# Loading the rests of strided tensors in pairs instead of one by one, in an attention and spectral mix kernel

## The chip, the core and the metric

The kernel runs on one core of a Trainium2 chip. A core has a matrix engine (TensorE, "PE" in the profile, its weight loads "PEld"), three engines for element-wise work (VectorE "DVE", ScalarE "ACT", GpSimd "POOL"), a queue engine (SyncE "SP") and 16 DMA engines that move data between the device memory and the on-chip memory. The metric is the device time of one execution in microseconds (us). Less is better.

## The reference

Three inputs q, k and v of 8 batches x 8 heads x 576 positions x 64 go through sparse attention. Heads 0 to 3 see a local window of 32 positions, heads 4 to 7 the earlier positions with the same remainder by 32 ("strided"):

```python
rel = pos[:, None] - pos[None, :]
mask_local = (rel >= 0) & (rel < stride)
mask_strided = (rel >= 0) & (pos[None, :] % stride == pos[:, None] % stride)
...
attn_out = softmax(masked scores) @ v
```

The result, taken as x of 8 x 576 x 512, is mixed along the positions in the frequency domain, with a complex 512 x 512 matrix for each of 64 modes, and then goes through a channel mix:

```python
X = np.fft.rfft(x, axis=1)
Yr = Xr @ w_r - Xi @ w_i      # for each of 64 modes
Yi = Xr @ w_i + Xi @ w_r
y = np.fft.irfft(Y, n=S, axis=1)
u = x + y
return u + np.maximum(u @ w_ch, 0.0)
```

The weights w_r and w_i are 2 x 64 x 512 x 512 numbers of four bytes, 134 MB; they are most of what is read.

## The kernel before

All loads of q, k, v and of the weights are issued from POOL's queue, in one order that the program writes out by hand; they turn four-byte numbers into two-byte ones on the way. The small constants come in over the queues of ACT and SP, and the output leaves over SP's, its last two pieces over ACT's.

The work has these stages:

1. Strided attention, batches 0 to 7 (loop at L751). Before batch b's scores, POOL issues some later loads: strided tensors with `load_str` (L219), local tensors with `load_loc` (L239), weights with `w_fetch` (L174). While a batch's scores and values run, `str_front` turns the next batch's q, k and v (L275, L291).
2. Local attention, batches 0 to 7 (loop at L780). Between its pieces stand the first 64 passes of the spectral mix, `mode(0, m)` (L542), which use one half of the channels.
3. The second half of the spectral mix, `mode(1, m)` for m from 0 to 57 (loop at L848), with pieces of the channel mix between the modes: `turn` (L588), `premix` (L637) and, by the sixteens, `spec` (L837).
4. The last six modes (loop at L959), then the tail: the rows of the output by `v_rows` and `u_rows`, summed on DVE and POOL and stored.

A strided tensor of one batch is 72 rows of 2048 numbers: 18 blocks for each of four heads, with the heads outermost. It lies in the on-chip buffer `ring`, in one of 12 slots: three tensors (v, q, k) for each of four batches. `load_str` loads them in pieces. The first 64 rows go in one transfer, for one batch (L229) or for two batches at once (L227). The remaining 8 rows, the "rest", are loaded for two batches when the even one is loaded. That makes twelve pairs of rests: v, q and k of batches 0 and 1, of 2 and 3, of 4 and 5, of 6 and 7. The condition at L233 counts them: the first five (v, q, k of batches 0 and 1, v and q of 2 and 3) are loaded as one transfer of 8 x 2 rows (L234), the other seven as two transfers of 8 rows (L237).

The weights of two modes come in two transfers, one for w_r and one for w_i, 128 rows of 2048 numbers each (L196); the last four modes come one by one (L199), as does one half of w_i for mode 0. There are five buffers for them in turn, and three more in places that other tensors take over. A pass of `mode` (L553) waits for its weights, and its fetch of later weights waits for a buffer. A transfer on POOL's queue is also issued only when the one eight places before it has landed.

Of the kernel before, what the change touches and what calls it, by code (L numbers as in the profile page):

```python
# [79 lines left out]
def kernel(  # L80
# [10 lines left out]
    nc = tc.nc  # L91
# [118 lines left out]
    SLOT = {2: 0, 0: 1, 1: 2}  # L210
# [8 lines left out]
    def load_str(b, nb):  # L219
        for vi in (2, 0, 1):  # L220
            n = 3 * (b % 4) + SLOT[vi]
            two = ring[:, n : n + 4 : 3, :]
            src = SRC[vi][b - b % 2 : b - b % 2 + 2, 4:8].rearrange(
                "b h (c r) d -> (h c) b (r d)", r=32
            )
            if nb == 2:
                nc.gpsimd.dma_start(two[0:64], src[0:64])  # L227
            else:
                nc.gpsimd.dma_start(ring[0:64, n, :], src[0:64, b % 2])  # L229

            if b % 2 == 0 and 3 * (b // 2) + SLOT[vi] < 5:  # L233
                nc.gpsimd.dma_start(two[64:72], src[64:72])  # L234
            elif b % 2 == 0:
                for j in range(2):
                    nc.gpsimd.dma_start(two[64:72, j], src[64:72, j])  # L237

    def load_loc(*bs):  # L239
        for b in bs:  # L240
# [461 lines left out]

    psum_pools(tp=3, sc=3, av=2)
    load_str(0, 1)
    const_load(nc.scalar, "cI", "cM6", "cM5", "cFs")
    load_str(1, 1)
    const_load(nc.sync, "cMl", "cFl", "cA")
    load_str(2, 2)
    w_fetch()

# [260 lines left out]
    for i in range(len(units)):  # L971
        v_rows(i)
        b, t = units[i]
# [42 lines left out]
```

## Time and profile before

| what | value |
| --- | --- |
| three runs, us | 439.85, 440.37, 439.7 (median 439.85) |
| the profiled execution, us | 439.85 |
| its span, first to last instruction, us | 438.1 |
| mean granted TensorE clock | 0.831 |
| busy: PE, DVE, ACT, POOL | 76%, 49%, 43%, 30% |
| moved by the DMA engines | 92.16 MB, 29107 packets |
| read from device memory | 163.22 MB |
| rests alone (L237) | 14 transfers of 32 KB, 6.5 to 15.0 us to landing, 11.2 in the median |
| rests in pairs (L234) | 5 transfers of 64 KB, 5.8 to 9.6 us to landing, 7.4 in the median |
| weights (L196) | 122 transfers of 512 KB, about 19 us to landing |

The profile cuts the span into 40 equal slices of 10.95 us. "GB/s" counts bytes as they are written, so half of what is read for the converted tensors. The line of DMA gives the mean busy share of the 16 engines in tenths. A landing is when all sixteen engines have reported that their part of a transfer is done; the trace keeps the time of each report, without the number of its engine. A line in the chain of waits names what was going on in the step that ended last: `DMA wt<-in_moe_w_i_dram` is a transfer of weights on its way, `PE y L553 x16` sixteen matmuls of a mode.

### The profile page before, as it was taken

How to read it: one execution, taken by the hardware profiler on the slowest of the kernel's cores; microseconds unless marked ns; L12 is line 12 of the kernel's file. 1: busy time of each engine (PE TensorE's matmuls, PEld its weight loads, DVE VectorE, ACT ScalarE, POOL GpSimd, SP SyncE). 2: the span in 40 equal slices, each digit the busy share in tenths (PEclk: the TensorE clock that was granted, in tenths of full speed). 3: DMA queues.
4: the chain of work that ended last, by engine and by line, in shares of the span. 5: the costliest groups of instructions: out<-in, count | busy, mean ns of one | idle time of the engine just before them, and what ended most of it. 6: DMA issues, size and time to landing. Idle time of an engine off the chain costs nothing.

```text
span 438.1 us, 12090 instructions
## 1 busy us (share of the span) xinstructions
PE 335.0 (76%) x5298; PEld 241.3 (55%) x5298; DVE 215.3 (49%) x466; ACT 188.1 (43%) x353; POOL 132.5 (30%) x215
## 2 busy tenths in 40 slices
PE   1986978779885878788874648577676859999994
PEld 1865766667664666666653335355444546655441
DVE  2788778844423243433511034335534535753895
ACT  1686678635442344345441302023322402442883
POOL 6433343323322222222222222222222222210893
PEclk9999899869786588788875558698978868989999
DMA  8999999999999999999999999999999999991687
GB/s 175 207 211 213 211 198 197 197 190 211 209 212 203 214 213 215 213 214 213 214 211 210 214 214 214 214 214 213 213 214 213 214 213 214 214 196 29 264 314 285
DMA packets 29107, 92.16 MB, mean 210 GB/s; under 512 B 4160, under 2 KB 5184, under 8 KB 29056
## 3 DMA queue, kind: packets, MB, share of 16 engines
q0 software_dynamic: 24816, 81.28, 95.0%
q1 hardware_dynamic: 3440, 9.46, 5.8%
q10 hardware_dynamic: 800, 0.67, 0.6%
q8 instruction: 41, 0.67, 0.6%
q14 instruction: 10, 0.08, 0.1%
HBM read 163.22 MB, written 9.44 MB: 394 GB/s over the span
## 4 chain that ended last, share of the span: by engine, by line
DMA 69%; PE 19%; DVE 5%; ACT 2%; issue 2%; POOL 1%; DVEq 0%; POOLq 0%
DMA wt<-in_moe_w_i_dram 49%; DMA wt<-in_moe_w_r_dram 10%; DMA ring<-in_k_dram 4%; DMA ring<-in_v_dram 3%; PE sc L651 3%; DMA ring<-in_q_dram 3%; PE y L553 3%; PE u L694 2%; PE v L694 2%; PE v L897 2%; DVE xb L256 1%; DVE kz L298 1%; PE tp L401 1%; PE tp L659 1%; ACT X L266 1%
## 5 line engine op out<-in xcount | busy, mean ns | idle before, releaser
L553 PE MATMUL y<-X,wt 128*128 128x16 f16 (+1 forms) x2048 | 82.3, 192 | 66.4 <-DMA wt<-in_moe_w_i_dram 65.2
L553 PEld LDWEIGHTS <-wt 128*128 128x128 f16 (+1 forms) x2048 | 72.4, 103 | 78.8 <-issue 56.2
L196 POOL DMA_DIRECT2D wt<-in_moe_w_r_dram x62 | 36.5, 588 | 131.1 <-PE y L553 51.0
L196 POOL DMA_DIRECT2D wt<-in_moe_w_i_dram x60 | 35.3, 588 | 75.4 <-DMA wt<-in_moe_w_i_dram 54.8
L660 ACT ACTIVATE v<-sc 128x512 f16<-128x512 f32 x32 | 19.1, 597 | 81.8 <-PE sc L651 81.7
L651 PE MATMUL sc<-w_cp,xT 128*128 128x512 f16 (+1 forms) x160 | 51.2, 445 | 1.8 <-DVE xT L623 1.8
L477 ACT ACTIVATE PL<-sc 128x480 f16<-128x480 f32 (+1 forms) x48 | 27.5, 579 | 50.7 <-PE sc L463 50.4
L255 DVE RECIPROCAL rec<-av 90x4 f32<-90x4 f32 (+2 forms) x80 | 14.6, 183 | 47.0 <-PE av L492 35.6
L256 DVE TENSOR_TENSOR xb<-av,rec 90x256 f16<-90x256 f32 (+2 forms) x80 | 36.0, 450 | 2.8
L661 DVE COPY xo<-tp 128x512 f16<-128x512 f16 x32 | 22.1, 692 | 29.9 <-PE tp L659 29.9
L408 DVE COPY qT<-tp 128x576 f16<-128x576 f16 x16 | 12.0, 757 | 41.4 <-PE tp L401 38.5
L401 PE MATMUL tp<-cI_s,ring 64*64 64x64 f16 x864 | 27.1, 213 | 2.5 <-issue 1.9
L266 ACT ACTIVATE v<-tp 128x640 f16<-128x640 f16 (+1 forms) x24 | 19.4, 807 | 21.8 <-PE tp L435 18.6
L366 ACT ACTIVATE PL<-sc 90x360 f16<-90x360 f32 (+1 forms) x48 | 22.8, 490 | 7.0 <-PE sc L359 6.1
L401 PEld LDWEIGHTS <-ring 64*64 64x64 f16 x864 | 21.3, 126 | 7.6 <-issue 4.8
L929 DVE TENSOR_TENSOR osb<-u,rl 128x512 f32<-128x512 f32 x36 | 23.6, 688 | 2.6 <-PE u L694 1.3
L603 DVE COPY xT<-tp 128x512 f16<-128x512 f16 x16 | 11.0, 689 | 28.1 <-PE tp L597 15.0
L266 ACT ACTIVATE kz<-tp 64x360 f16<-64x360 f16 (+1 forms) x32 | 19.0, 593 | 11.5 <-PE tp L401 10.1
L912 POOL TENSOR_TENSOR rl<-rl,xo 128x512 f32<-128x512 f32 x16 | 18.3, 1159 | 18.2 <-ACT rl L910 17.9
L447 PE MATMUL sc<-cMl_s,cI_s 128*128 128x480 f16 (+1 forms) x48 | 22.5, 469 | 1.6 <-ACT X L266 1.6
L651 PEld LDWEIGHTS <-xT 128*128 128x128 f16 (+1 forms) x160 | 14.5, 108 | 16.2 <-issue 4.6
L463 PE MATMUL sc<-qT,kz 128*128 128x160 f16 (+1 forms) x160 | 22.4, 267 | 0.3 <-issue 0.3
(106 smaller groups left out, 655.7 us busy)
## 6 DMA issues: line engine op xcount, KB each, us to landing
wt<-in_moe_w_r_dram POOLq DMA_DIRECT2D x62, 512.0 KB, 18.9
wt<-in_moe_w_i_dram POOLq DMA_DIRECT2D x60, 512.0 KB, 19.4
out_dram<-osb SPq DMA_DIRECT2D x14, 512.0 KB, 2.7
ring<-in_v_dram POOLq DMA_DIRECT2D x8, 288.0 KB, 13.9
ring<-in_q_dram POOLq DMA_DIRECT2D x8, 288.0 KB, 13.8
ring<-in_k_dram POOLq DMA_DIRECT2D x8, 288.0 KB, 13.4
ring<-in_v_dram POOLq DMA_DIRECT2D x3, 512.0 KB, 14.6
ring<-in_q_dram POOLq DMA_DIRECT2D x3, 512.0 KB, 14.6
```

The source lines that it names most:

```text
L196: nc.gpsimd.dma_start(dst, rows)
L256: nc.vector.tensor_tensor(out=dst, in0=val.rearrange("p h (q c) -> p h c q", c=4), in1=rec[0:n, 0:pieces] .to_broadcast((n, pieces, 64)) . ...
L266: nc.scalar.activation(out=out, in_=in_, func=ACTF.Copy)
L366: nc.scalar.activation(out=PS[0:n, ds(POFF[t], 4 * n)], in_=scp[0:n, 0 : 4 * n], func=ACTF.Exp, scale=SCALE,)
L401: nc.tensor.transpose(tp[ds(64 * hp, 64), ds(64 * i, 64)], qn[ds(64 * hp, 64), ds(64 * (9 * g + i), 64)], idn[ds(64 * hp, 64), ds(64 * hp, ...
L447: nc.tensor.matmul(scp[:, 0 : n * times].rearrange("p (h x) -> p h x", h=times), idn, mask_rows("cMl", n, times), start=True, stop=False,)
L463: nc.tensor.matmul(scp[:, ds(col, n)], kzs[par][:, hp, ds(s0, 128)], qTs[par][:, ds(s0, n)], start=False, stop=(i == len(todo) - 1),)
L477: nc.scalar.activation(out=dst, in_=src, func=ACTF.Exp, scale=SCALE)
L553: nc.tensor.matmul(yv[:, mi, e, :], wt[pr, XC[c], ds(128 * e, 128)], Xh[half][pr, c, :, :, m], start=(c == 0), stop=(c == 3),)
L651: nc.tensor.matmul(vp[pr, :], xT[:, ch, cols], w_chs["cp"][:, ch, :], start=(ch == 0), stop=(ch == 3),)
L661: nc.vector.tensor_copy(out=xo[pr].rearrange("p (h q c) -> p h q c", h=2, c=4), in_=tp[pr, 0:512].rearrange("p (h c q) -> p h q c", h=2, c=4),
L929: nc.vector.tensor_tensor(out=osb[:, t % 2, :], in0=up, in1=rls[b, t][:, t % 2, :], op=AluOp.add)
```

## The change

`load_str` no longer loads any rests one by one: each of the twelve pairs is one transfer of 8 x 2 rows. For the first five nothing changes. For the other seven (k of batches 2 and 3, and v, q and k of 4 and 5 and of 6 and 7) one instruction on POOL's queue stands where two stood. The rows and their places in `ring` are the same, and so is the order of all other instructions on every engine.

```diff
@@ -227,14 +227,8 @@
                 nc.gpsimd.dma_start(two[0:64], src[0:64])
             else:
                 nc.gpsimd.dma_start(ring[0:64, n, :], src[0:64, b % 2])
-            if b % 2 == 0 and 3 * (b // 2) + SLOT[vi] < 5:
+            if b % 2 == 0:
                 nc.gpsimd.dma_start(two[64:72], src[64:72])
-            elif b % 2 == 0:
-                for j in range(2):
-                    nc.gpsimd.dma_start(two[64:72, j], src[64:72, j])
```

## The prediction

> **What bounds the kernel now.** I read the page from the top, then the chain of waits in order of time, then the moved bytes around the changed transfers. The page:
>
> ```profile
> PEclk9999899869786588788875558698978868989999
> DMA  8999999999999999999999999999999999991687
> GB/s 175 207 211 213 211 198 197 197 190 211 209 212 203 214 213 215 213 214 213 214 211 210 214 214 214 214 214 213 213 214 213 214 213 214 214 196 29 264 314 285
> q0 software_dynamic: 24816, 81.28, 95.0%
> q8 instruction: 41, 0.67, 0.6%
> DMA 69%; PE 19%; DVE 5%; ACT 2%; issue 2%; POOL 1%; DVEq 0%; POOLq 0%
> ```
>
> POOL's queue q0 keeps the 16 DMA engines at 9 tenths or more until slice 35, at a flat 214 GB/s: the stream of weights paces the kernel. The chain says until when (start, length, what):
>
> ```profile
> 319.70 19.38 DMA wt<-in_moe_w_i_dram
> 339.36 20.34 DMA wt<-in_moe_w_i_dram
> 359.83 0.64 PE y L553 x16
> ...
> 376.04 0.86 PE sc L651 x4
> ...
> 387.12 1.71 PE sc L651 x4
> ```
>
> Before 359.83 each step is a landing; after it TensorE hardly waits. Its waits from 360 on hold one for a weight, and that one ends at 359.83:
>
> ```profile
> PE y L553 <- DMA wt<-in_moe_w_i_dram: 2.9, 1, 2.9
> ```
>
> So the time is when the weights issued at 339.36 have landed, plus 78 us of TensorE, VectorE and ScalarE work. Anything that brings that landing forward shortens the kernel, as long as the last weights also come earlier.
>
> **Who lands last.** A transfer has landed when all its engines are done, and the trace holds sixteen stamps for each, one per DMA engine. I sorted those of the strided loads of batches 6 and 7 into the earlier and the later eight (us):
>
> ```
>                       issued   first eight      last eight
> v, 64 rows a batch     44.67   55.84 - 57.05    58.05 - 59.26
> v, rest, batch 6       46.66   56.02 - 57.22    58.35 - 59.55
> v, rest, batch 7       47.18   56.19 - 57.38    58.67 - 59.85
> q, 64 rows a batch     47.70   58.38 - 59.59    61.16 - 62.31
> k, rest, batch 7       59.55   61.26 - 62.35    64.88 - 66.09
> weights                60.05   65.12 - 65.60    67.39 - 68.52
> ```
>
> From one 64-row transfer to the next the last eight take 3.11 us (58.05 to 61.16), the first eight 2.54. The packet records show why: of a rest loaded alone (8 rows) eight engines carry one 4 KB packet each, the other eight only the 4-byte stamp, and it is the same eight (call them A, the others B) for both rests of a pair and for v, q and k. Back to back, a row costs its engine 0.305 us and a stamp behind a row 0.022. Six pairs of rests (twelve rows) put A behind B by 12 x (0.327 - 0.01) = 3.8 us; the means of the two eights at the last rest's stamps differ by 3.74, so the halves were level at 23 us.
>
> For a pair loaded as one (L234), the packets of the second and third pair (q and k, batches 0 and 1) show eight engines with two rows each, and for the third pair the other eight: they alternate. Level at 23 us is what this gives if A is the half of pairs 2 and 4: 4 rows, plus 2 for the first rests alone, against 6.
>
> Two more things decide the end. First, B has run dry once, since POOL could not issue: each issue waits until the transfer eight places earlier has landed, which A delays.
>
> ```profile
> 54.70 0.61 POOL L227 DMA_DIRECT2D ring<-in_k_dram  x1 [2.25 <-DMA wt<-in_moe_w_r_dram]
> 56.86 0.52 POOL L237 DMA_DIRECT2D ring<-in_k_dram  x1 [1.56 <-DMA wt<-in_moe_w_i_dram]
> 59.55 0.51 POOL L237 DMA_DIRECT2D ring<-in_k_dram  x1 [2.17 <-DMA ring<-in_v_dram]
> 60.05 0.61 POOL L196 DMA_DIRECT2D wt<-in_moe_w_r_dram  x1
> ```
>
> The moved bytes from 56 to 70 us, in 0.35 us steps, sag at 60.5 to 63.5:
>
> ```profile
> GB/s 211 258 211 211 199 199 199 199 211 234 222 222 187 141 129 187 141 152 199 152 187 199 211 187 187 258 234 211 199 246 187 176 208 214 221 206 222 204 190 223
> ```
>
> The gap of the means falls from 3.74 to 2.70 by the weights' stamps: B lost 1.04 us there. Second, each of the 41 instruction fetches on q8 (16 KB) sets one engine back by about 1.35 us, in a round of eight engines. Followed from stamp to stamp, two of them are in A and six in B. Relative to the quickest engine, the transfer that ends the wait at 359.83 has A's two at 7.82 and 6.43 us and the latest of B at 5.47; in the last transfer of the stream (393.00 to 399.10) A's two stand at 6.10 and 5.70, the latest of B at 4.90. One engine of A sets the end.
>
> **The change, part by part.** In seven pairs (k of batches 2 and 3, all of 4 to 7) two POOL transfers of 8 rows become one of 2 x 8 rows. Bytes, rows, the order of all other instructions and the queues of SP and ACT stay. Removed: seven issues on POOL's queue.
>
> - POOL's time: 7 x about 0.52 us (rows of L237), against 7 x about 0.08 more for the wider issue (0.60, row of L234). POOL is 30% busy and waits for landings around these lines (rows above), so this is worth nothing by itself.
> - A: 14 x 0.327 = 4.58 us go; with alternation going on, pairs 6, 8, 10 and 12 fall to A, 4 x 0.61 + 7 x 0.022 = 2.59 come. Net -1.98. If the seven began on B, A would get three: -2.6.
> - B: 3 x 0.61 + 0.15 - 0.14 = +1.84; with four pairs +2.45. The dry spell goes if it comes from A's lag and the places the rests take: -1.04; at the other end it stays: 0. I take -1.04, since the issues just before it wait for landings 2.2 us each, and two transfers in place of three then stand in the same eight places. So +0.80, bounds +0.80 and +2.45.
> - A pair lands when two rows of one engine are in, not one: 0.305 us later on its eight. The first compute that such a load holds up is L275 on q of batch 6, released at 62.64 by A's last stamp. By alternation that pair falls to B, which by then has carried three pairs: 59.94 + 6 x 0.305 = 61.8. So it comes earlier, not later, and the lag on A covers the wider pair.
>
> Sum at 359.83: A 7.82 - 1.98 = 5.84, B 5.47 + 0.80 = 6.27: the latest engine moves from 7.82 to 6.27, so 1.55 earlier, and B is now last. At the stream's end: A 4.12, B 5.70 against 6.10, 0.40 earlier; TensorE starts the last mode at 400.14, 1.04 after its weights landed, so it can start up to 1.44 earlier. The smaller counts: -1.45. The profiled execution took 439.85 us (span 438.1, 1.75 around it), which is also the median of the three runs: 438.4.
>
> [...]
>
> **The rivals.**
>
> *The gain stays in B.* B takes four pairs, or its dry spell stays. Then B at 359.83 is 5.47 + 1.41 = 6.88 (four pairs) or 7.31 (three, dry): 0.94 or 0.51 earlier; at the end 0.83 or 0.40 after the slack of 1.04: 439.0 or 439.45. Both together: 7.92 and 7.35, so 0.1 to 0.2 late: 440.05. For it: B has six of the engines that fetches delay. Against: the gap fell just where the bytes sag.
>
> *Slower: the granted clock in the last 78 us.* TensorE is busy 39.9 of the 42 us from 360 to 402, at a mean clock of 0.90 there (0.75 from 106 to 360). The chain shows the price: four L651 passes take 1.71 us at half clock (387.12) and 0.86 at full. A half-clock stretch of the clock record, 3.4 us, costs 1.7 us. From two such stretches more the change loses: +3.4 - 1.45 = +1.95, 441.8; one more gives 440.1. For it: the clock drops in short stretches all along, and moved work meets them elsewhere. Against: the work itself is the same, and three runs agree within 0.7 us.
>
> *A's lag alone counted.* If B's fetches fall elsewhere or B gains more, the full 1.98 arrives: 437.9.
>
> *The rests are not what they seem*, that is, a pair is again carried as single rows on A: no row changes its engine, only seven stamps go: 439.7. The second and third pair speak against it.
>
> **How the numbers follow.** Forecast, 437.7 to 439.2 around 438.4: 0.43. Gain kept by B or the pair carried as before, 438.9 to 440.2: 0.30. Full gain: 0.07. Slower by the clock, from 440.8: 0.20. The three runs span 0.15%, so I call 0.2% (0.88 us) the least that can be told from no change: faster is below 438.97, slower above 440.73. Faster: 0.40 of the forecast, 0.07, 0.02 of B's case: 0.49. Slower 0.21, the rest 0.30. The range, 437.0 to 441.0, takes in every case but the two-stretch clock and stray gains there.
>
> **What would show it.** Right: the later eight no longer fall behind through the strided loads (the two halves within 1 us at 61 us instead of 3.74); no sag below 190 GB/s at 60 to 63; the wait at L553 that ended at 359.83 ends near 358.3; the last weights land near 398.7. Wrong in its first step if the halves still part by 3 us; in its second if the sag stays; in its third if the landing comes earlier and TensorE's work after it takes longer than 78 us, with more half-clock stretches. A landing later than 359.7 would break the whole argument.

## The result, and the profile after

| | before | after |
| --- | --- | --- |
| median, us (runs) | 439.79 (439.7 to 440.37, 4) | 434.65 (433.94 to 435.15, 4) |
| ratio after to before, 95% interval | | 0.9879 (0.9861 to 0.9897) |
| profiled execution, us; its span | 439.85; 438.1 | 434.99; 433.2 |
| TensorE's wait for the weights of a mode ends, us | 359.83 | 355.07 |
| from there to the end of the span, us | 78.3 | 78.1 |
| last weights landed, us | 399.10 | 394.32 |

The change saves 5.3 us (4.5 to 6.1 by the interval), over three times the forecast 1.45. The direction was right, the size far off: 434.65 lies under the range.

The page of the changed kernel, the lines that answer to the first ones of the prediction:

```profile
PEclk9999799958997565985965559597969688989999
GB/s 174 203 210 214 213 213 211 212 210 212 214 213 213 213 213 214 213 214 214 214 212 213 213 214 213 214 214 213 214 213 214 213 214 213 213 193 37 267 318 288
q0 software_dynamic: 24704, 81.28, 94.7%
DMA 59%; PE 26%; DVE 7%; issue 3%; ACT 3%; POOL 0%; DVEq 0%; POOLq 0%
```

As many bytes, 112 packets fewer (seven stamps on sixteen engines). The row to read is GB/s: slices 6 to 9 (55 to 99 us) now stand at 213 211 212 210, where they were 198 197 197 190. From slice 14 on the two rows nearly agree. The chain of waits around the landing that sets the end (start, length, what):

```profile
315.79 19.48 DMA wt<-in_moe_w_i_dram
335.27 0.28 issue
335.55 19.38 DMA wt<-in_moe_w_i_dram
354.93 0.14 issue
355.07 0.64 PE y L547 x16
```

It has the same shape as before, 4.76 us earlier. TensorE's one wait for a weight from 355 to 402 us is as long as it was (L547 is the L553 of before):

```profile
PE y L547 <- DMA wt<-in_moe_w_i_dram: 3.1, 1, 3.1
```

And the moved bytes from 56 to 70 us have lost their sag:

```profile
GB/s 211 211 211 199 211 234 246 199 211 211 176 199 222 246 211 211 211 199 199 199 234 234 222 187 211 211 187 246 234 222 187 206 195 238 207 203 187 208 211 211
```

Where the time came from is read off a table by stages: a stretch, its length, the busy times of PE, PEld, DVE, ACT and POOL with the instructions they began, then PE's granted clock, the DMA engines' busy share and GB/s. The kernel before, then the changed one:

```profile
60.00:62.70 2.70, 1.13 (x23) 0.79 (x20) 2.38 (x7) 1.62 (x4) 1.25 (x3) 1.00 0.98 168
62.70:106.00 43.30, 36.44 (x741) 30.30 (x742) 28.81 (x70) 26.39 (x54) 15.01 (x27) 0.88 1.12 198
106.00:140.00 34.00, 24.75 (x537) 19.91 (x534) 11.43 (x22) 12.95 (x26) 9.79 (x17) 0.80 1.09 208
140.00:355.00 215.00, 157.14 (x2654) 113.23 (x2653) 78.52 (x160) 71.25 (x127) 50.58 (x86) 0.75 1.07 213
```

```profile
60.00:62.70 2.70, 2.38 (x45) 1.73 (x42) 2.56 (x7) 2.44 (x6) 1.05 (x3) 1.00 1.05 209
62.70:106.00 43.30, 35.84 (x718) 29.36 (x718) 29.60 (x74) 26.09 (x55) 13.46 (x25) 0.84 1.09 211
106.00:140.00 34.00, 26.19 (x620) 21.11 (x618) 13.40 (x26) 16.00 (x30) 10.70 (x19) 0.92 1.07 213
140.00:355.00 215.00, 160.29 (x2628) 114.71 (x2626) 78.64 (x161) 68.99 (x123) 50.70 (x86) 0.72 1.06 213
```

By rates: 2.7 x (1 - 168/209) = 0.5 us in the dry spell, 43.3 x (1 - 198/211) = 2.7 us in the stage in which local tensors (L244, in the changed kernel L238) and weights are loaded in turn, 34 x (1 - 208/213) = 0.8 us behind it: 4.0 of the 4.76 us by 140 us, nothing afterwards. The rest is where the last engine stands beside the mean: at the landing that ends the wait, the last of the sixteen stamps is 4.0 us behind their mean before and 3.4 after. So most of the gain lies in a stage that the change doesn't touch at all: the last transfer that it edits is issued at 59.55 us before and at 51.56 after.

The busy share of the DMA engines is the clue: before, they were busier in that stage (1.12 against 1.09) and moved less. A packet itself took longer. The records of single packets show it. An undisturbed 4 KB packet (a row of weights or of a strided tensor) takes 324 ns, a packet of 2304 bytes (a local tensor's) 192 ns. From 65 to 140 us, counted as slow above 400 and 250 ns:

```
                 4096 bytes       2304 bytes       excess over 324 / 192 ns
before           240 of 1933      278 of 3072      5.05 us an engine
after              9 of 2107       17 of 3072      0.20 us an engine
```

All 3072 packets of 2304 bytes fall into this window in both kernels. Of the 4 KB packets 174 fewer got through before: 0.71 MB, or 3.3 us of the stream at 213 GB/s. (Both traces hold all 17984 of them, so none is missing.) The slow packets come in bouts of one to 2.5 us in which nearly all engines are slow at once, at 70, 73 to 75.5, 79 to 81, 88 to 90 and 93 to 95.5 us. Between 74 and 75 us the median is 522 ns for 4 KB and 335 ns for 2304 bytes, and all engines together move 146 GB/s. All bouts fall into stretches where one half of the engines, two to four microseconds ahead, is already on the next kind of row. But not all of such a stretch is slow: from 67 to 69, 71 to 73 and 77 to 79 us packets of both kinds also run side by side, and 7 of 418 are slow. What had to be found was why the lag of one half makes packets slow.

### The profile page after: what moved, and what is told of

It reads as the page before. It is cut to its first block, busy times and chain, and to the rows that moved or that the text cites. A ratio compares the mean times of both kernels' runs of the same rounds, so it can differ in the third digit from the quotient of the medians.

```text
span 433.2 us, 12081 instructions
## 1 busy us (share of the span) xinstructions
PE 337.0 (78%) x5298; PEld 241.4 (56%) x5298; DVE 215.6 (50%) x466; ACT 188.1 (43%) x353; POOL 129.2 (30%) x208
## 4 chain that ended last, share of the span: by engine, by line
DMA 59%; PE 26%; DVE 7%; issue 3%; ACT 3%; POOL 0%; DVEq 0%; POOLq 0%
DMA wt<-in_moe_w_i_dram 48%; DMA wt<-in_moe_w_r_dram 5%; PE y L547 4%; DMA ring<-in_q_dram 4%; PE sc L645 3%; DMA ring<-in_k_dram 2%; PE v L688 2%; PE u L688 2%; PE v L891 2%; PE tp L395 2%; PE sc L514 2%; DVE kz L292 1%; DVE xb L250 1%; PE sc L441 1%; DMA ring<-in_v_dram 1%
## 5 line engine op out<-in xcount | busy, mean ns | idle before, releaser
L547 PE MATMUL y<-X,wt 128*128 128x16 f16 (+1 forms) x2048 | 82.9, 192 | 58.6 <-DMA wt<-in_moe_w_i_dram 57.4
L547 PEld LDWEIGHTS <-wt 128*128 128x128 f16 (+1 forms) x2048 | 73.1, 103 | 72.2 <-issue 66.9
L645 PE MATMUL sc<-w_cp,xT 128*128 128x512 f16 (+1 forms) x160 | 52.8, 456 | 1.5 <-DVE xT L617 1.5
L395 PE MATMUL tp<-cI_s,ring 64*64 64x64 f16 x864 | 26.0, 208 | 1.9 <-issue 1.1
L395 PEld LDWEIGHTS <-ring 64*64 64x64 f16 x864 | 20.3, 121 | 7.3 <-issue 4.4
L457 PE MATMUL sc<-qT,kz 128*128 128x160 f16 (+1 forms) x160 | 23.3, 273 | 0.1
```

The source lines that it names most:

```text
L395: nc.tensor.transpose(tp[ds(64 * hp, 64), ds(64 * i, 64)], qn[ds(64 * hp, 64), ds(64 * (9 * g + i), 64)], idn[ds(64 * hp, 64), ds(64 * hp, ...
L457: nc.tensor.matmul(scp[:, ds(col, n)], kzs[par][:, hp, ds(s0, 128)], qTs[par][:, ds(s0, n)], start=False, stop=(i == len(todo) - 1),)
L547: nc.tensor.matmul(yv[:, mi, e, :], wt[pr, XC[c], ds(128 * e, 128)], Xh[half][pr, c, :, :, m], start=(c == 0), stop=(c == 3),)
L645: nc.tensor.matmul(vp[pr, :], xT[:, ch, cols], w_chs["cp"][:, ch, :], start=(ch == 0), stop=(ch == 3),)
```

## The experiments

Ratios are to the kernel before, run beside it, with the 95% interval. GB/s by stages and slow packets (the two kinds added, 65 to 140 us) are from one profiled execution each. That of e1a_half_a (439.94 us, median 436.47) is the longest of its seven runs; that of e2_three (441.81 us) is the longest of ten and not among those behind its ratio, so its row can't be set beside 0.9923.

| run | ratio | 60-65 | 62.7-106 | 106-140 | slow packets |
| --- | --- | --- | --- | --- | --- |
| before | 1 | 181 | 198 | 208 | 518 |
| after | 0.9879 (0.9861-0.9897) | 212 | 211 | 213 | 26 |
| e1a_half_a | 0.9928 (0.9899-0.9958) | 175 | 210 | 213 | 27 |
| e1b_half_b | 0.9993 (0.9964-1.0021) | 175 | 198 | 207 | 573 |
| e1c_turns | 0.9990 (0.9959-1.0022) | 119 | 203 | 213 | 43 |
| e2_three | 0.9923 (0.9890-0.9955) | 209 | 201 | 208 | 471 |
| e4b_apart_before | 0.9980 (0.9957-1.0003) | 174 | 204 | 206 | 346 |
| e4a_apart_after | 0.9876 (0.9843-0.9908) | 213 | 211 | 214 | 24 |
| e5b_order_before | 1.0018 (0.9990-1.0045) | 179 | 196 | 212 | 437 |
| e2_twelve | 1.0038 (1.0012-1.0065) | 169 | 196 | 212 | 423 |
| e8_swap_before | 0.9923 (0.9900-0.9947) | 179 | 209 | 214 | 29 |
| e8a_swap_half_a | 1.0091 (1.0055-1.0128) | 186 | 192 | 208 | 677 |
| e9_places_before | 0.9922 (0.9901-0.9943) | 180 | 208 | 213 | 32 |
| e7_heads_before | 1.0003 (0.9985-1.0021) | 168 | 195 | 211 | 577 |
| e10_spread_before | 0.9967 (0.9937-0.9996) | 184 | 208 | 213 | 37 |
| e10a_spread_half_a | 0.9952 (0.9921-0.9983) | 176 | 209 | 213 | 37 |

### Which half lags

By the packets of the second and third pair in the kernel before, pairs loaded as one take turns between the halves of the engines. If a small transfer of the same form (8 x 2 rows of 32 bytes, 512 bytes in place of 64 KB) uses up a turn too, the changed kernel can be made to put all seven new pairs on one half, without a single row loaded alone. The three kernels differ only in the place of these small transfers: behind each of the seven pairs, ahead of each, or two behind each (which keeps the turns as they were):

```diff
+    bump_t = big.tile([128, 20, 2, 16], F16, name="bump")
+    bumps = []
+
+    def bump(src):
+        i = len(bumps)
+        bumps.append(i)
+        nc.gpsimd.dma_start(bump_t[64:72, i], src[64:72, :, 0:16])
...
                 nc.gpsimd.dma_start(two[64:72], src[64:72])
+                if 3 * (b // 2) + SLOT[vi] >= 5:
+                    bump(src)
```

> The changed kernel, with a small transfer (8 x 2 rows of 16 numbers, into a place that nothing reads) issued after each of the seven pairs in question. If pairs take turns between the halves, each small one uses up a turn, and all seven pairs fall on half A, as the fourteen rests loaded alone did. Skew theory (the halves drift apart, and then run slower than their rows cost): the gap of the halves at 61 us is back at 3.5 to 4.5 us, the moved bytes from 62 to 98 us fall from 211 to about 198 GB/s, time 438.5 to 441. Load theory (only A's own rows count, as the prediction had it): A has 6 rows more than now, 2.0 us, time 436 to 437. Places theory (each transfer takes one of eight places on POOL's queue): as many transfers as before the change, time 439 to 441 with or without a gap.

> As the run with the small transfer after each pair, but with it before each pair, so that all seven pairs fall on half B, which has six of the eight engines that instruction fetches delay. Skew theory: a gap of 3.5 to 4.5 us the other way round, 438.5 to 442, and the last weights later by B's own rows on top. Load theory: B gains 8 rows, 2.4 us: 436.5 to 437.5. Places theory: the same as the run before it, 439 to 441.

> The changed kernel with two small transfers after each of the seven pairs, so that the pairs take turns again, with 21 transfers where the kernel before had 14 and the changed one 7. Skew theory: no gap (within 1 us at 61 us), 211 GB/s from 62 to 98 us, time 434 to 436. Load theory: the same, 434.5 to 435.5. Places theory: slower than the kernel before, 440 to 444.

The stage from 62.7 to 106 us, with the small transfer behind each pair:

```profile
62.70:106.00 43.30, 36.08 (x631) 29.48 (x630) 28.76 (x72) 25.49 (x53) 15.06 (x27) 0.76 1.09 210
```

and ahead of each pair:

```profile
62.70:106.00 43.30, 35.19 (x711) 29.15 (x711) 28.37 (x69) 25.41 (x53) 14.99 (x27) 0.88 1.12 198
```

Both have the gap of the halves back (the first weights behind the rests land on eight engines at 65.9 to 66.1 us and on the others at 67.3 to 69.7; in the second at 65.3 to 66.2 and 67.8 to 68.7), and both have the dry spell at 60 to 65 us (175 GB/s). Only the second has slow packets (573 against 27), just as before has, and it costs 2.9 us more than the first by the ratios, 3.9 by the medians (440.38 against 436.47 us). In the profiled executions the landing that ends TensorE's wait lies 3.1 us apart, first in e1a, then in e1b:

```profile
337.38 19.54 DMA wt<-in_moe_w_i_dram
357.05 0.64 PE y L556 x16
```

```profile
339.71 20.33 DMA wt<-in_moe_w_i_dram
360.17 0.64 PE y L556 x16
```

That this execution of e1a still took 439.94 us comes from what follows the landing: 81.1 us against 78.4 in e1b, at a granted clock of 0.82 from the landing to 399 us, against 0.90 up to 402 us in e1b. So a gap alone didn't make packets slow here; which half was late did. The half of e1b is that of the rests loaded alone, A. And in e1a, where every new pair takes the turn that the first of them has in the changed kernel, it is B: I had the turns the wrong way round, and the name of that run with them. The stamps of the landing that ends the wait bear this out. By the prediction, fetches delay two engines of A and six of B. In before and in e1b the last two of the sixteen stand apart, 6.43 and 7.82, 6.56 and 8.22 us behind the first, as A's two would; in e1a the last six do, 5.95 to 7.82 us behind the first, with two more at 4.41 and 4.77, as B's six and A's two would.

The turns kept with two small transfers show a third thing, POOL's eight places. Hardly a slow packet (43), and yet no gain (0.9990): 14 more transfers stand in the queue, each issue waits about 2 us for a landing eight places back, and the engines run dry (a busy share of 0.67 from 60 to 65 us, 1.05 from 20 to 60):

```profile
54.50 0.56 POOL L238 DMA_DIRECT2D ring<-in_q_dram  x1 [1.58 <-DMA wt<-in_moe_w_i_dram]
56.97 0.55 POOL L179 DMA_DIRECT2D bump<-in_q_dram  x1 [1.90 <-DMA wt<-in_moe_w_r_dram]
59.47 0.55 POOL L179 DMA_DIRECT2D bump<-in_q_dram  x1 [1.96 <-DMA wt<-in_moe_w_i_dram]
62.36 0.59 POOL L234 DMA_DIRECT2D ring<-in_k_dram  x1 [2.33 <-DMA ring<-in_v_dram]
```

Four transfers in eight microseconds here, a pair of rests, two tiny ones and one of 64 rows: 119 GB/s from 60 to 65 us, 201 from 20 to 60. A transfer's place cost something here even when its bytes didn't, where small ones stood close together.

### The dose

The condition at L233 with another bound: only the last three pairs loaded alone (9 in place of 5), or all twelve (0).

```diff
-            if b % 2 == 0 and 3 * (b // 2) + SLOT[vi] < 5:
+            if b % 2 == 0 and 3 * (b // 2) + SLOT[vi] < 9:
```

> The kernel before with only the last three pairs (batches 6 and 7) loaded one by one: the condition's 5 becomes 9. Skew theory: a gap of about 1.9 us at 61 us, less than one transfer of weights takes (2.46 us), so the slow stretches between weights and local loads are short: 435 to 437. Load theory: three sevenths of 2 us, 435.3 to 435.9. Places theory: three sevenths of 5.1 us, 436.5 to 437.2.

> All twelve pairs of rests loaded one by one: the other end of the dose (the kernel before has seven, the changed kernel none). A carries ten rows more alone and the pairs' turns are gone. If A's rows alone decide, A gets 24 rows against 14 and four or six in pairs: the halves part by 6 to 7.6 us at 61 us, the end is 1.5 to 2.5 us later than before by A's rows, and every meeting of weights and local loads lasts longer. Theory (slow packets on top): the rate from 62.7 to 106 us falls under 198, to 190 to 196, and the time rises by 2 to 5 us, ratio 1.005 to 1.012. Rival (the slow packets come from the pairs and singles standing mixed, not from the lag): 205 GB/s or more and a ratio under 1.005.

No pair alone, three, seven, twelve: 0.9879, 0.9923, 1, 1.0038. The time rises with the number, but not the way I had it. With twelve the gap of the halves was 3.8 us at 61 us (means 62.5 and 66.3 at the last rest), as with seven, not 6 to 7.6, perhaps since the early half had nothing left to run ahead with (169 GB/s from 60 to 65 us), and the slow packets were no more than with seven. With three, the runs went from 434.8 to 441.8 us, and the profiled one was the longest of them (441.81 us, with 471 slow packets); what the shorter ones looked like inside isn't known. This dose says that the order is right, and nothing finer.

### Where weights and local loads meet

The two weight tiles that stand between the local loads moved behind them, in the kernel before and, as a control, in the changed one:

```diff
-        w_fetch([2, 1, 1, 1, 1, 1, 0, 0][b])
+        w_fetch([2, 1, 1, 1, 0, 0, 0, 2][b])
```

> The kernel before, with the two weight tiles that stood between the local loads (one behind the local tensors of batch 0, one behind those of batches 1 and 2) moved behind those of batch 5. The fourteen rests stay alone, so the half A still lags by about 3.7 us at 61 us. Theory (packets run slow where one half of the engines is still on weights and the other already on local tensors): such meetings fall from six to two between 60 and 106 us, so most of the 4.6 us that an engine loses there to slow packets goes; the rate of the local stage (62.7 to 106 us) rises from 198 to 205 GB/s or more, and the time falls by 2.5 to 3.5 us, to about 437 (ratio 0.992 to 0.995). Rival 1 (local loads are slow whenever A lags, whatever stands beside them): 198 GB/s as before and a ratio within 0.002 of 1. Rival 2 (the lag alone costs the time, the slow packets don't reach the end): the rate rises, but the ratio stays within 0.002 of 1.

> The changed kernel with the same move of two weight tiles, as the control of the run before it. Its halves are level and its packets are never slow, so the theory has nothing to gain: the time of the changed kernel, ratio 0.986 to 0.990 to the kernel before, 211 GB/s from 62.7 to 106 us. If the move by itself were worth something (buffers, places in the queue), this run would show it too: a ratio under 0.985 or over 0.991.

Of the moved bytes of e4b this is the row to look at:

```profile
GB/s 175 209 211 207 211 192 204 211 202 200 207 211 211 213 214 214 214 215 213 214 205 214 213 214 213 214 213 214 214 214 214 213 214 213 214 184 13 264 313 285
```

The bouts went with the meetings: between 72 and 92 us, where there are now local tensors alone, hardly a packet is slow (211 GB/s in slice 8, 77 to 88 us), and at 95 to 112 us, where weights follow, there are new bouts (slices 9 and 10: 202, 200). The ratio is worth 0.9 us only, not 2.5 to 3.5, and its interval takes in no change at all. By rates the stage to 106 us gained 1.3 us (204 in place of 198 GB/s) and the one behind it gave back 0.3 (206 in place of 208): the later meetings still cost, which I hadn't counted. Taken alone this run also fits its rival 2, slow packets that don't reach the end; e8 and e9 below rule that out. The control stayed at the changed kernel's time. So, by the places of the bouts, slow packets belong to the meeting of weights and local tensors with A late.

With every batch's tensors issued as q, k, v in place of v, q, k nothing changed:

```diff
-        for vi in (2, 0, 1):
+        for vi in (0, 1, 2):
...
-            for vi in (2, 0, 1):
+            for vi in (0, 1, 2):
```

> The kernel before, with every batch's tensors issued as q, k, v in place of v, q, k, strided and local ones alike; the first five pairs of rests in one are still counted v, q, k of batches 0 and 1, v and q of batches 2 and 3, and A still lags. Theory (the meeting of weights with local loads makes packets slow, whichever tensor stands there): slow packets of 400 to 550 ns between 65 and 95 us again, 196 to 200 GB/s there, ratio 0.997 to 1.003. Rival (one tensor's place in memory makes the slow packets): the bouts move or go; with none left 211 GB/s and a ratio near 0.99. Whatever waits for v first in a batch can come later by up to 2 us in the first batches; this is not on the path that ends last.

196 GB/s and 437 slow packets, with a ratio that holds 1: no single tensor is to blame.

### The places on the chip

The code of `w_fetch` gives the next idea. A transfer of w_r fills partitions 0 to 63 of a tile, two modes each, one of w_i partitions 64 to 127; a local tensor fills all 128. If the one half of the engines carries the lower 64 rows of a local tensor and the other the upper, then with one half late, eight engines that are still on w_i and eight already on a local tensor write to the same 64 partitions, or they don't, by which half is late. Three edits, one for each way to turn this: the order of the two matrices, their places, and the addresses in the device memory.

```diff
-            for ri, src in enumerate((moe_w_r, moe_w_i)):
+            for ri, src in ((1, moe_w_i), (0, moe_w_r)):
```

> The kernel before with the two transfers of every weight tile in the other order: w_i (to partitions 64 to 127) first, then w_r (to partitions 0 to 63). Theory (places on the chip): a local tensor goes to all 128 partitions, A carrying the lower half of them and B the upper; with A late, A is still on w_i (upper) when B is on the local tensor's upper half, and on the local tensor's lower half when B is already on w_r (lower), so all sixteen engines write to the same 64 partitions and packets run slow. With the order turned, the two halves always write to different partitions: no slow packets after 65 us, 210 GB/s from 62.7 to 106 us in place of 198, ratio 0.990 to 0.993 as with the lag on B (0.9928). Rival (the lag of A alone, or which tensors are read together): slow packets and 198 GB/s as before, ratio 0.997 to 1.003.

> The kernel with the seven pairs on one half and a small transfer after each, in which B lags and no packet was slow (ratio 0.9928), now with w_i ahead of w_r in every weight tile. Theory (places on the chip): with B late, the turned order makes the two halves meet on the same 64 partitions: slow packets of 450 to 550 ns come up, 200 GB/s or less from 62.7 to 106 us in place of 210, ratio 0.997 to 1.003. Rival (slow packets only where A lags): none, 210 GB/s, ratio 0.993 as without the turn.

```diff
-                dst = wt[ds(64 * ri, 64)]
+                dst = wt[ds(64 * (1 - ri if m else ri), 64)]
```

> The kernel before with the places of the two weights exchanged from mode 1 on, w_r to partitions 64 to 127 and w_i to 0 to 63, and the order of the transfers kept; the modes then compute with exchanged weights. In the device memory the same things are read in the same order as before, on the chip the order of the places is turned. Theory (places on the chip): no slow packets, 210 GB/s from 62.7 to 106 us, ratio 0.990 to 0.993, the same as with the order turned. Rival (which addresses of the device memory are read together): slow packets as before, 198 GB/s, ratio 0.997 to 1.003.

```diff
-                    SRC[vi][b, 0:4].rearrange("h (cb i) d -> (h cb) (i d)", i=18),
+                    SRC[vi][b, 3:7].rearrange("h (cb i) d -> (h cb) (i d)", i=18),
```

> The kernel before with its local loads reading heads 3 to 6 in place of 0 to 3, so other addresses of the device memory (442 KB further) to the same places on the chip; the local attention then computes on other heads. Theory (places on the chip): as before, slow packets between 65 and 95 us, 196 to 200 GB/s from 62.7 to 106 us, ratio 0.998 to 1.002. Rival (addresses of the device memory that fall together with those of the weights): the slow packets go or change much, 205 GB/s or more, ratio near 0.992.

The stage from 62.7 to 106 us in the kernel before with the order turned, then the same for the kernel with the lag on B:

```profile
62.70:106.00 43.30, 35.85 (x691) 29.35 (x689) 28.85 (x72) 25.93 (x54) 15.07 (x27) 0.80 1.08 209
```

```profile
62.70:106.00 43.30, 34.96 (x641) 28.68 (x641) 29.08 (x74) 25.73 (x55) 13.87 (x25) 0.84 1.13 192
```

The same edit takes the slow packets away where A lags (518 to 29, ratio 0.9923) and brings them up where B lags (27 to 677, 0.9928 to 1.0091, more than I had put down). Exchanging the places with the order of reading kept does the same as turning the order (0.9922, 32 slow packets):

```profile
62.70:106.00 43.30, 36.02 (x637) 29.32 (x635) 28.94 (x73) 25.87 (x54) 15.07 (x27) 0.76 1.09 208
```

Reading other addresses does nothing (1.0003, 577). So it is the places that count, not what is read. And the fourteen rests alone, a gap of the halves and the dry spell (179, 180 GB/s) are all still there in e8 and e9: what the slow packets cost is 1 - 0.9923, or 3.4 us (2.3 to 4.4). The gap is a little smaller there, 2.9 and 2.8 us at the last rest against 3.7, so up to 0.9 us of this could be the smaller lag; that was not separated.

One thing remained: do the halves have to meet on the same 64 partitions, or is it something else about the two matrices? Each weight transfer was spread over all 128 partitions, one row each, so that, by the same idea, each half stays in its own places whichever lags:

```diff
                 elif i < 2 * NM - 4:
+                    if m:
+                        dst = wt[:, ri].rearrange("p c e -> p (c e)")
+                        rows = src[m].rearrange("(p c) e -> p (c e)", c=4)
                     nc.gpsimd.dma_start(dst, rows)
                     continue
```

> The kernel before with every weight transfer from mode 2 on spread over all 128 partitions, as the local tensors are: 128 rows of one matrix go to one row each, in place of 64 partitions with two rows each. As many transfers, rows and bytes; the modes then compute with weights in the wrong places. A still lags. Theory (packets are slow where the two halves of the engines write to the same 64 partitions, one half a weight's rows, the other a local tensor's): each half now always writes to its own 64 partitions, so no packet after 65 us is slow, 209 GB/s from 62.7 to 106 us, ratio 0.990 to 0.994 as with the order turned (0.9923). Rival (it is not the places but which of the two matrices stands next to the local tensors, or two kinds of rows in flight at once): slow packets as before, 198 GB/s, ratio 0.997 to 1.003.

> The kernel with the seven pairs on one half and a small transfer after each, where B lags (ratio 0.9928, no slow packets), with every weight transfer spread over 128 partitions likewise. Theory (meeting on the same 64 partitions): each half keeps to its own places, whichever lags: no slow packets, 209 to 210 GB/s from 62.7 to 106 us, ratio 0.991 to 0.995. Rival (spreading the weights only turns the sign, as the turned order did: slow packets with the lag on B): 192 to 200 GB/s and a ratio of 1.000 to 1.009.

With the lag on A, then on B:

```profile
62.70:106.00 43.30, 35.33 (x635) 28.88 (x635) 28.59 (x72) 25.62 (x54) 14.92 (x29) 0.81 1.09 208
```

```profile
62.70:106.00 43.30, 34.60 (x694) 28.59 (x693) 28.77 (x72) 25.89 (x54) 14.27 (x27) 0.88 1.09 209
```

37 slow packets in either. (The spread transfers also read other rows of the two matrices; e7 moved the addresses of the local tensors only.) The gain of the stage arrives, the one of the time only in part (0.9967, not 0.990 to 0.994; with the lag on B 0.9952, just outside 0.991 to 0.995): in e10 198 of 1961 packets are now slow from 20 to 60 us (32 in before), 2.5 us an engine, where spread weights stand next to strided rows in partitions 0 to 63. The meeting has moved to an earlier stage. That fits, but no run of its own tested it.

## Why the prediction was right and wrong

- *The stream of weights paces the kernel up to one landing, then come 78 us of work.* Right: the landing came at 355.07 us, and 78.1 us followed it. So the rival *Slower: the granted clock in the last 78 us* fell: that part is 0.2 us shorter.
- *"at a flat 214 GB/s".* This is the step that failed. The row that I quoted beside these words says 198 197 197 190 in slices 6 to 9, and I passed over it; the packets of a local tensor are smaller, and I let that explain it. The changed kernel runs the same local tensors at 211. My sum took every row at 0.305 us in all stages and counted only rows that change engines; the term that is missing is the stream's rate between 65 and 140 us, which hangs on the lag. It is worth 3.4 us (e8, e9, and, at 3.3 us, the 174 rows that the stream before fell behind), over twice my whole sum. What sets it is the half that lags (27 slow packets in e1a, 573 in e1b), together with the places of the rows that then meet (29 in e8, 677 in e8a, 32 in e9).
- *Rests alone all fall to A, A lags by 3.74 us, and B ran dry because of it.* The halves: right, and shown by e1b, which makes nearly the same lag (4.2 us) and the same time with pairs alone. In the changed kernel the sixteen stamps of the last strided transfer run from 62.71 to 64.89 us without a step between two groups; the means of the earlier and the later eight are 1.2 us apart, against 3.74, a little over the 1 us that the prediction named. The dry spell: gone, as taken (212 against 181 GB/s).
- *"pairs 6, 8, 10 and 12 fall to A".* Wrong: e1a shows that the turn of pair 6 is B's, so B takes four and A three. By the counts in the prediction this makes A -2.6 and B +1.41, 0.94 us earlier and not 1.55. It mattered little, since the halves come out within 1.2 us either way. By the prediction's count this turn gives A eight rows and B four up to 23 us, which doesn't fit level halves there; that stays open.
- *The sum, 1.45 us.* What the changed kernel gains beyond e8, where rows, gap and dry spell stand and only the slow packets are gone, is 0.9923 - 0.9879, or 1.9 us. With an interval of 1.3 us on either side it agrees with 1.45 and with 0.94, and can't tell them apart. So nothing here speaks against the size of this term, and it was the smaller of two: 1.9 + 3.4 = 5.3 us.
- *The rivals and the range.* *The gain stays in B* had the right number of pairs for B (four) and the wrong outcome; *The rests are not what they seem* fell with the halves coming out level. None of the rivals, nor *A's lag alone counted*, had a price for a change in the rate of the stream, so the range, 437.0 to 441.0, was made from the same incomplete list as the forecast.
- *POOL's seven issues cost nothing by themselves.* Open: e1c shows that many small transfers do run the stream dry through the eight places (119 GB/s), so some of the 1.9 us may be places and not rows. They were not separated.

## What to carry to other kernels

Before a stage's rate is put down to the size of its packets, compare the duration of one packet of each size with the same size elsewhere: busy engines that move fewer bytes (a DMA share of 1.12 with 198 GB/s against 1.09 with 211) had slow packets here, and there was something to gain. When transfers of a few rows make one half of the DMA engines late, look at what the halves then do side by side: here its company cost 3.4 us, and the lag, the dry spell and the places on POOL's queue together 1.9. Where the lag can't be removed, the order of the transfers can be turned: issuing w_i ahead of w_r in the kernel before is one line and gives 0.9923.

## What the runs showed of the hardware that was not expected

- Where weights and local tensors met with one half of the engines late, so that by the inference below eight engines wrote a weight's rows and eight a local tensor's to the same 64 partitions, packets were slow: in the kernel before, 4 KB packets go from 324 to mostly 420 to 560 ns (median of the slow packets 481), 2304-byte packets from 192 to mostly 260 to 345 ns (308), all engines together down to 138 GB/s (80 to 81 us). The slow packets went or came with the order and the places of the transfers (518 to 29 in e8, 27 to 677 in e8a, 518 to 32 in e9), and with the weights spread over all partitions there were 37 with either lag (e10, e10a). A weight transfer, with sixteen stamps, goes to 64 partitions as well, and the stream of them runs at 213 GB/s from 140 to 355 us, its 4 KB packets at 324 ns in the median. What within the 64 places makes the difference was not found, nor why the first part of a meeting runs at full speed; the trace has no addresses of packets. That A carries the lower half of a local tensor is inferred from the runs that turn the sign, not seen.
- A transfer of 8 x 2 rows of 32 bytes switched the turn of the next one, as the stamps show (the last two late in e1b, the last six in e1a), and so decided 2.9 us by the ratios, 3.9 by the medians.
